# Windowed attention with an FFN behind it: global rows of two head pairs in one pass, early w_in sums column by column, loads on a second queue

## The chip, the cores and the metric

The kernel runs on one core of a Trainium2 chip. Its time is the device time of one execution in microseconds (us); lower is better. A core has a matrix engine (TensorE, PE in the profile), three engines for elementwise work (VectorE or DVE, ScalarE or ACT, GpSimd or POOL) and SyncE (SP), which here only issues DMAs. ScalarE can issue DMAs too, in its own stream of instructions; the profile calls that part of the stream ACTq. Results of TensorE land in eight PSUM banks.

## The reference

For 8 batches and 8 heads of dimension 64 there are 512 local and 32 global tokens. Scores are scaled by 1/8. A global token attends to all 544 keys, a local one to the 32 global keys and to local keys at most 32 positions away:

```python
s_g = scale * np.matmul(q_g, k_all.transpose(0, 1, 3, 2))
out_g = np.matmul(sm(s_g), v_all)
s_ll = np.where(np.abs(pos[:, None] - pos[None, :]) <= 32, s_ll, -1e9)
out_l = np.matmul(sm(np.concatenate([s_lg, s_ll], -1)), np.concatenate([v_g, v_l], 2))
...
x = attn_out.transpose(0, 2, 1, 3).reshape(B * S, H * D)     # 4352 x 512
h = x @ w_in                                                  # 512 x 2048
out = (h - np.tanh(h)) @ w_out                                # 2048 x 512
```

sm subtracts the row's maximum, exponentiates and divides by the row's sum (plus 1e-9). The weights arrive as 64-bit floats.

## The kernel before

**How the order is made.** Every piece of work is an operation of the class `Order` (L51): a function that emits instructions, the engines it may run on with a duration for each, the keys it reads and writes, the banks it takes, and a due time. `Order.run` places the operations one after another on a model of the engines and emits the instructions in the order of their planned starts. The due times come from a table of numbers (`CFG`), with a shift for single operations (`NUDGE`), a preference for one engine (`CHOICE`) and a delay (`HOLD`). The chip's own time is not known to it; on the chip each engine goes through its list in order and waits on semaphores. Where the plan has TensorE wait, before about 72 us of its own clock, it puts in filler matmuls (L1947), small and of no use for the result, which keep TensorE's clock up.

**The stages.** Batch 0's attention runs first, by pairs of heads (class `Pair`, pairs 0 to 3). For a pair, queries and keys are loaded as rows (L620), turned by TensorE (L636) and copied out of PSUM (L449): keys in windows into `first_kw`, queries into `first_q`, with the global keys put between (copies from `first_g`). Then come the scores of the 64 global rows of the pair (L669, L670), their peak on VectorE (L674, a sum with a mask and a minimum), exponentials on ScalarE (L679, L680), the inverse of the sum on VectorE (L458, L459) and the scaling on POOL. The local rows follow in windows: scores (L731), peak on VectorE (L1234), exponentials on ScalarE (L1241), scaling on POOL (L808), turning (L751), copies into `keys_first`, and the product with the values (L827), whose result is split in a high and a low part `x_hi`, `x_lo` for one column block of 128 features per pair.

From batch 1 on (class `WindowPair`, pair 4 and later) scores are made in another layout (L964, L980), with peak L1057, exponentials L1065, turning L1118. The FFN of a batch is interleaved with the attention of the next. One of its 16 steps makes 128 hidden columns: `x @ w_in` as three products of parts (hi·hi, lo·hi, hi·lo), each of four matmuls of 128x512 (L1294), then tanh on ScalarE, subtraction on VectorE, a split in parts, and four output tiles from `w_out` (L1342). After the last batch only the rest of the FFN runs.

**The weights.** They are loaded in 512 KB pieces of 64-bit floats into staging tiles (`stage`, `wpair`, `first_q`, and half pieces into `first_kw`; L521), rebuilt into 32 bits by ScalarE (L528) and VectorE (L532, L536), and split into a high part (a cast, L449) and a low part (POOL, L542). This runs beside batch 0's attention and the first steps of the FFN.

**The queues.** All loads are issued by SP, but for one half of pair 0's keys and of its queries, which ScalarE issues (L620). Each load takes the next of eight completion counters (DMAHW0 to DMAHW7 in the order's rows) and waits for the load that had that counter before.

## Time and profile before

| | us |
|---|---|
| median of 3 runs | 903.67 |
| lowest and highest | 902.84, 904.29 |
| profiled execution | 905.04 |
| its span, first to last instruction | 903.2 |

| engine | busy us | share of the span | instructions |
|---|---|---|---|
| PE (matmul) | 887.3 | 98% | 7678 |
| DVE | 648.7 | 72% | 2309 |
| ACT | 406.1 | 45% | 1186 |
| POOL | 321.0 | 36% | 511 |

The shares are means over stages that differ. TensorE's share hides what its busy time holds: fillers count as busy. The granted clock of TensorE is 0.998 over the span. The views used below are the busy time by stretches, the timelines of the engines, groups of instructions by line and shape, and the chain of waits, which goes back from the last instruction from each step to what released it.

### The profile page before, as it was taken

Reading aid. Unit: us, or ns where it says so; the run is one execution under the profiler, and the core shown is the slowest. Engines: PE = TensorE matmul, PEld = TensorE weight load, DVE = VectorE, ACT = ScalarE, POOL = GpSimd, SP = SyncE. Lnnn points to the kernel's source line nnn. Section 1 sums busy time; section 2 is a strip of 40 time slices with the busy share of each in tenths; the row PEclk is TensorE's granted clock in tenths of the full one; section 3 lists DMA queues with packets and bytes.
Section 4 is the critical chain, followed back from the end, with each engine's and each line's share of the span. In section 5 each row is a group of like instructions: output and inputs, shape, how many; then the busy total and the mean of one; then the engine's idle time right before and its main releaser. Section 6 shows DMA issues by size and latency. Waiting matters only on the chain.

```text
span 903.2 us, 21527 instructions
## 1 busy us (share of the span) xinstructions
PE 887.3 (98%) x7678; PEld 733.1 (81%) x7678; DVE 648.7 (72%) x2309; ACT 406.1 (45%) x1186; POOL 321.0 (36%) x511
## 2 busy tenths in 40 slices
PE   7899999999999999999999999999999999999998
PEld 5678878888888888888888888888888888899886
DVE  5997867776667757577775757577775758787773
ACT  6985656533334334334444334334444343443332
POOL 6677665433333413333333323333333323000000
PEclk9999999999999999999999999999999999999999
DMA  9766646533324323333333323333333210100001
GB/s 225 190 179 183 189 107 150 128 66 60 71 51 108 70 47 68 92 66 71 66 66 94 63 49 71 86 73 64 65 65 100 55 29 15 47 1 0 1 1 70
DMA packets 266058, 72.20 MB, mean 80 GB/s; under 512 B 250592, under 2 KB 259296, under 8 KB 265952
## 3 DMA queue, kind: packets, MB, share of 16 engines
q1 hardware_dynamic: 264752, 70.44, 34.2%
q8 instruction: 61, 1.00, 0.5%
q10 hardware_dynamic: 1200, 0.39, 0.2%
q14 instruction: 45, 0.37, 0.1%
HBM read 61.87 MB, written 8.91 MB: 78 GB/s over the span
## 4 chain that ended last, share of the span: by engine, by line
PE 90%; DMA 2%; DVE 2%; issue 2%; POOL 2%; ACT 1%; SPq 0%; POOLq 0%; DVEq 0%; ACTq 0%
PE bank L1342 32%; PE bank L1294 31%; PE bank L1664 7%; PE bank L1784 6%; PE bank L1151 6%; PE bank L964 3%; PE bank L980 1%; DMA wpair<-in_moe_w_out_dram 1%; PE bank L1690 1%; DMA first_q<-in_moe_w_in_dram 1%; PE bank L1947 1%; POOL w_out_lo L542 0%; DVE first_q L536 0%; POOL w_in_lo L542 0%; DMA first_raw<-in_k_l_dram 0%
## 5 line engine op out<-in xcount | busy, mean ns | idle before, releaser
L1311 POOL TENSOR_TENSOR glo<-t,ghi 128x512 fp32r<-128x512 f32 x112 | 146.4, 1307 | 285.2 <-PE bank L1342 260.7
L1096 DVE STREAM_TRANSPOSE keys_first<-prob 32x256 f32<-32x256 f32 x384 | 167.3, 436 | 8.0 <-POOL prob L1078 1.3
L1302 ACT ACTIVATE t<-bank 128x512 f32<-128x512 f32 x112 | 66.8, 596 | 164.6 <-PE bank L1294 163.3
L1305 DVE TENSOR_TENSOR t<-bank,t 128x512 f32<-128x512 f32 x112 | 76.5, 683 | 79.2 <-ACT t L1302 77.8
L449 ACT CAST ghi<-t 128x512 fp32r<-128x512 f32 (+1 forms) x122 | 74.8, 613 | 114.6 <-PE bank L1342 95.5
L1342 PE MATMUL bank<-w_out_hi,glo 128*128 128x512 f32 x448 | 124.9, 393 | 0.0
L1342 PE MATMUL bank<-w_out_lo,ghi 128*128 128x512 f32 x448 | 124.9, 393 | 0.0
L1342 PE MATMUL bank<-w_out_hi,ghi 128*128 128x512 f32 x448 | 123.5, 390 | 0.0
L1294 PE MATMUL bank<-x_hi,w_in_hi 128*128 128x512 f32 x448 | 119.9, 390 | 0.9 <-ACT w_in_hi L449 0.9
L1294 PE MATMUL bank<-x_hi,w_in_lo 128*128 128x512 f32 x448 | 120.0, 390 | 0.1
L1294 PE MATMUL bank<-x_lo,w_in_hi 128*128 128x512 f32 x448 | 120.0, 389 | 0.1
L1078 POOL TENSOR_SCALAR prob<-prob,st 128x128 f32<-128x128 f32 x224 | 81.8, 387 | 106.9 <-ACT prob L1065 90.9
L1057 DVE CUSTOM_DVE_ANT_0 prob<-bank,wraw 128x128 f32<-128x128 f32 x224 | 53.6, 286 | 89.5 <-PE bank L964 88.7
L1342 PEld LDWEIGHTS bank<-w_out_lo,ghi 128*128 128x128 f32 x448 | 83.0, 188 | 20.8 <-issue 4.3
L1342 PEld LDWEIGHTS bank<-w_out_hi,glo 128*128 128x128 f32 x448 | 83.0, 188 | 20.4 <-issue 3.7
L1294 PEld LDWEIGHTS bank<-x_hi,w_in_hi 128*128 128x128 f32 x448 | 83.7, 188 | 19.2 <-ACT w_in_hi L449 1.4
L1294 PEld LDWEIGHTS bank<-x_lo,w_in_hi 128*128 128x128 f32 x448 | 84.1, 188 | 17.9 <-DVE x_lo L838 0.5
L1342 PEld LDWEIGHTS bank<-w_out_hi,ghi 128*128 128x128 f32 x448 | 83.9, 188 | 18.0 <-issue 0.3
L1294 PEld LDWEIGHTS bank<-x_hi,w_in_lo 128*128 128x128 f32 x448 | 83.9, 188 | 18.0 <-POOL w_in_lo L542 0.6
L1065 ACT ACTIVATE prob<-prob,st 128x128 f32<-128x128 f32 x224 | 87.7, 399 | 2.6 <-DVE st L1057 1.3
L449 ACT CAST x_hi<-bank 128x256 fp32r<-128x256 f32 x59 | 19.4, 376 | 95.4 <-PE bank L980 93.6
L1151 PEld LDWEIGHTS bank<-keys_first,values 128*64 128x64 f32 x784 | 49.2, 138 | 9.9 <-DVE t L1305 7.8
(234 smaller groups left out, 1382.9 us busy)
## 6 DMA issues: line engine op xcount, KB each, us to landing
rawkq<-in_q_l_dram SPq DMA_DIRECT2D x112, 64.0 KB, 2.2
rawkq<-in_k_l_dram SPq DMA_DIRECT2D x112, 64.0 KB, 2.3
out_dram<-wpair SPq DMA_DIRECT2D x28, 256.0 KB, 2.1
values<-in_v_l_dram SPq DMA_DIRECT2D x28, 120.0 KB, 2.3
keys_first<-in_v_l_dram SPq DMA_DIRECT2D x28, 120.0 KB, 2.6
stage<-in_moe_w_out_dram SPq DMA_DIRECT2D x6, 512.0 KB, 3.9
wpair<-in_moe_w_out_dram SPq DMA_DIRECT2D x6, 512.0 KB, 4.4
first_q<-in_moe_w_in_dram SPq DMA_DIRECT2D x6, 512.0 KB, 4.9
```

Source lines behind the costliest of these rows:

```text
L449: (nc.scalar.copy if e == "A" else nc.vector.tensor_copy)(dst, src)
L1065: nc.scalar.activation(x, x, AF.Exp, bias=s[:, k:k + 1], scale=-1.0, accum_out=s[:, 8 + k:9 + k])
L1078: nc.gpsimd.tensor_scalar(x, x, s[:, k:k + 1], 1.0, op0=ALU.mult, op1=ALU.mult)
L1096: nc.vector.transpose(view(win_kf[W * k:W * k + W], [(CH, 2), (P, NT), (1, W)], 3 * G + W * i), src)
L1151: nc.tensor.matmul(dst, win_values[h][:, window(b)], src, start=n == 0, stop=n == len(parts) - 1, skip_group_check=True)
L1294: nc.tensor.matmul(self.h[s][:, j * n:(j + 1) * n], w[:, cc, f * P:(f + 1) * P], self.x()[xi][:, cc, :n], start=part == 0 and cc == 0 and ...
L1302: nc.scalar.activation(tt_[q], self.h[s], AF.Tanh)
L1305: nc.vector.tensor_sub(tt_[q], self.h.pop(s), tt_[q])
L1311: eng[e].tensor_sub(gg[q][1], tt_[q], f32(gg[q][0]))
L1342: nc.tensor.matmul(self.acc[tt], g[:, j * self.n + tt * P:j * self.n + (tt + 1) * P], low_out(f) if wi else high_out(f), start=s == 0 and ...
L1664: nc.tensor.matmul(self.hold(tt, tags), g(), low_out(f) if wi else high_out(f), start=first and k < len(tts), stop=last and k == len(mms) - 1)
L1784: nc.tensor.matmul(dst[:, at], w, m, start=fresh and n == 1, stop=n == 6, skip_group_check=True)
```

## The change

Three things change in what is computed when, and all the tables of the planner.

1. **Global rows of two pairs at once.** Pairs 0 and 1, and pairs 2 and 3, share one pass: both are turned first, their scores go to the two halves of the rows of the same two banks, and peak, exponentials, inverse and scaling are done once on 128 rows instead of twice on 64.
2. **Early sums.** For the first three steps of batch 0's FFN the twelve matmuls are not ordered by part but by column block: three matmuls for each pair, as soon as that pair's part of x is there. Two of the three take a bank of the group "acc" (4 to 7) instead of "h" (0 to 3).
3. **A second queue.** Loads of keys and queries of pairs 1 to 3, of values of batch 0 and of weights may be issued by ScalarE's queue as well; the planner chooses.

Line numbers move by up to 36: L636 becomes L648, L669 L683, L731 L749, L827 L845, L964 L982, L980 L998, L1118 L1136, L1294 L1340 for the early sums, L1947 L1983, L521 L533, L528 L540.

```diff
+    AHEAD = 3
-    CFG = dict(win=-59.4186, a_g=0.122, a_kg=0.185, a_ph=0.0132, a_qs=11.4846, a_w=0.0464, a_wn=0.0881, a_xg=7.3446, d_g=0.2172,
+    CFG = dict(win=-838.608, a_g=0.7258, a_kg=0.0055, a_ph=0.2148, a_qs=0.9626, a_w=0.056, a_wn=2.3603, a_xg=7.3446, d_g=0.7129,
...
+    def queue(e):
+        return nc.scalar if e == "A" else nc.sync
+
+    def queues(d):
+        return [("S", d), ("A", d + 0.15, CFG["a_ld"])]
...
-                nc.sync.dma_start(raw.bitcast(I32).rearrange("p (a c) k -> p a (c k)", a=a), src)
+                queue(e).dma_start(raw.bitcast(I32).rearrange("p (a c) k -> p a (c k)", a=a), src)
...
-        add(("S", 0.37), load, due, w=keys, res=spare, xfer=0.9 * N / 256)
+        add(queues(0.37), load, due, w=keys, res=spare, xfer=0.9 * N / 256)
...
-                add(("S", 0.95), load(a, (k_l, q_l)[a]), self.due(self.C["o_ld"] - 8), w=[self.key[a]], xfer=1.3)
+                add(queues(0.95) if self.j else ("S", 0.95), load(a, (k_l, q_l)[a]), self.due(self.C["o_ld"] - 8), w=[self.key[a]], xfer=1.3)
...
         def add_global_scores(self):
+            i = 2 * self.j
+            two = (self, pairs[self.j + 1])
...
+            def mm(x):
+                def fn(e, tags):
+                    if x is self:
+                        box["s0"], box["s1"] = bank([P, 256], tags[names[0]]), bank([P, 320], tags[places[0]])
+                    rows, kw = slice(64 * x.u, 64 * x.u + 64), first_kw[x.set]
+                    q = first_gq[:, x.jj].rearrange("p h g -> p (h g)")
+                    nc.tensor.matmul(box["s0"][rows], q, kw[:, :256], start=True, stop=True)
+                    nc.tensor.matmul(box["s1"][rows], q, kw[:, KG:KG + 320], start=True, stop=True)
+                return fn
...
-                for c0, c1, src, low, k in ((0, 256, box["s0"][rows], view(first_mask[rows], [(0, 256)]), 20), (256, 576, box["s1"][rows], first_mask[rows], 21)):
+                for c0, c1, src, low, k in ((0, 256, box["s0"], view(first_mask, [(0, 256)]), 20), (256, 576, box["s1"], first_mask, 21)):
...
+            early = s < AHEAD and self.name == "b0"
+
+            def column(cc):
+                def fn(e, tags):
+                    if cc == 0:
+                        self.h[s] = bank([P, 512], tags[hk])
+                    for wi, xi in ((0, 0), (0, 1), (1, 0)):
+                        nc.tensor.matmul(self.h[s], (w_in_hi, w_in_lo)[wi][:, cc, s * P:(s + 1) * P], self.x()[xi][:, cc, :n],
+                                         start=cc == 0 and wi + xi == 0, stop=cc == NCC - 1 and wi == 1)
+                return fn
+
+            for cc in range(NCC * early):
+                r = [k + (xi,) for k in self.xkeys if k[2] // 2 == cc for xi in range(2)] + [("w", "i", s, j, wi) for j in range(2) for wi in range(2)]
+                last = cc == NCC - 1
+                add(("T", 0.68), column(cc), due + 0.1 * cc - CFG["ahead"] * (not last), r=r, w=[hk],
+                    res=[tk] if last else (), alloc=[(hk, "acc" if s < 2 else "h")] if cc == 0 else ())
...
     def attention(j):
         p = pairs[j]
-        p.add_turn()
-        p.add_global_scores()
+        if j % 2 == 0:
+            p.add_turn()
+            pairs[j + 1].add_turn()
+            p.add_global_scores()
```

The order changes everywhere in the first part of the program; over the whole of it TensorE has 92 fillers before and 52 after. Three places follow. In the rows the line comes first, then the operation, out<-in and the shape of the result, in brackets the engines or completion counters waited for (Activation is ScalarE), and x4 is a row four times.

ScalarE's list from the start of the program to the first exponentials of a window (L1241), before; L528 is the rebuilding of a weight piece, L679 the exponentials of pair 0's global rows:

```order
L620 DMA first_raw<-in_k_l_dram 128x4x64
L620 DMA first_raw<-in_q_l_dram 128x4x64
L449 ACT_TABLE_LOAD
L449 COPY first_g<-bank_96 128x128 [waits PE_49]
...
L449 COPY first_kw<-bank_97 128x2x96 [waits PE_49]
L449 COPY first_kw<-first_g 128x2x2x32 [waits Activation_49]
L449 COPY first_kw<-first_g 128x2x2x32
L528 ACTIVATE stage<-stage 128x512 [waits DMAHW2_49]
L679 ACTIVATE pg<-pg,st_91 64x32 [waits DVE_49]
...
L1241 ACTIVATE t_67,st_91<-t_67,st_91 128x224 [waits DVE_49] x2
```

And after, where those are L1259:

```order
L632 DMA first_raw<-in_k_l_dram 128x4x64
...
L533 DMA wpair<-in_moe_w_out_dram 128x1024
L632 DMA first_raw<-in_k_l_dram 128x4x64
L632 DMA first_raw<-in_k_l_dram 128x4x64 [waits DMAHW0_49]
...
L455 COPY first_g<-bank_96 128x128 [waits PE_49]
...
L533 DMA first_q<-in_moe_w_in_dram 128x4x256 [waits DMAHW0_49]
L533 DMA stage<-in_moe_w_in_dram 128x4x256 [waits DMAHW3_49]
L455 COPY first_kw<-first_g 128x2x2x32 [waits Activation_49]
L1274 DMA values<-in_v_l_dram 96x3x64 [waits DMAHW5_49]
L1274 DMA values<-in_v_l_dram 96x3x64 [waits DMAHW6_49]
L1276 DMA values<-in_v_g_dram 32x6x64 [waits DMAHW7_49]
L1259 ACTIVATE t_67,st_91<-t_67,st_91 128x224 [waits DVE_49] x2
```

Five loads stand ahead of the first copy, two more ahead of the copy of pair 0's global keys (`first_kw<-first_g`), three loads of values ahead of the first exponentials; the second copy for pair 0 went to VectorE, and the exponentials of the global rows come later.

TensorE's list at the start, from the last turn of pair 0 (the queries) on, before; L669 and L670 are pair 0's global scores, L636 turns pair 1's keys, L731 makes window scores:

```order
L636 MATMUL bank_98<-idr,first_raw 128x128 [waits DMAHW5_49,DMAHW2_49]
...
L669 MATMUL bank_99<-first_kw,first_m 64x256 [waits DVE_49,Activation_49]
L670 MATMUL bank_100<-first_kw,first_m 64x320
L636 MATMUL bank_101<-idr,first_raw 128x128 [waits DMAHW1_49,DMAHW0_49]
...
L731 MATMUL bank_102<-first_kw,first_q 128x224 [waits DVE_49]
...
```

And after, the same work at L648, L683, L684 and L749:

```order
L648 MATMUL bank_98<-idr,first_raw 128x128 [waits DMAHW7_49,DMAHW2_49]
...
L683 MATMUL bank_99<-first_kw,first_m 64x256 [waits DVE_49,Activation_49]
L684 MATMUL bank_100<-first_kw,first_m 64x320
L749 MATMUL bank_101<-first_kw,first_q 128x224 [waits DVE_49]
...
L648 MATMUL bank_97<-idr,first_raw 128x128 [waits DMAHW6_49,DMAHW0_49]
...
L648 MATMUL bank_98<-idr,first_raw 128x128 [waits DMAHW2_49,DMAHW1_49]
...
L683 MATMUL bank_99<-first_kw,first_m 64x256 [waits DVE_49]
L684 MATMUL bank_100<-first_kw,first_m 64x320
...
```

The window scores of pair 0 now come ahead of pair 1's turns, and pair 1's global scores directly behind these, in the same two banks as pair 0's.

TensorE's list from pair 4's last global scores (L980) to the turn of its probabilities (L1118), before; L827 is the last product of batch 0, L1294 the sums of the FFN's first steps:

```order
L980 MATMUL bank_98<-first_m,win_gq 32x192
L827 MATMUL bank_102<-keys_first,values 64x160 [waits DMAHW2_49,DMAHW0_49]
...
L1947 MATMUL bank_97<-mask_88 128x224
L1294 MATMUL bank_97<-x_hi_85,w_in_hi 128x512 x3
L1294 MATMUL bank_97<-x_hi_85,w_in_hi 128x512 [waits Activation_49]
L1294 MATMUL bank_96<-x_hi_85,w_in_hi 128x512 [waits DVE_49]
L1294 MATMUL bank_96<-x_hi_85,w_in_hi 128x512 x3
...
L1294 MATMUL bank_97<-x_hi_85,w_in_lo 128x512 x4
L1294 MATMUL bank_96<-x_lo_86,w_in_hi 128x512 x4
L1118 MATMUL bank_98<-idr,prob 128x64 [waits Pool_49]
```

And after, with L998, L845, L1340 and L1136 for them; the second product of the two stands among the sums:

```order
L998 MATMUL bank_98<-first_m,win_gq 32x192
L1340 MATMUL bank_103<-x_hi_85,w_in_hi 128x512
L1340 MATMUL bank_103<-x_lo_86,w_in_hi 128x512 [waits DVE_49]
...
L1340 MATMUL bank_98<-x_hi_85,w_in_hi 128x512 [waits DVE_49,Activation_49]
...
L1340 MATMUL bank_98<-x_hi_85,w_in_lo 128x512 [waits Pool_49]
L845 MATMUL bank_100<-keys_first,values 64x160 [waits DMAHW5_49,DMAHW3_49]
...
L1340 MATMUL bank_98<-x_hi_85,w_in_hi 128x512
L1340 MATMUL bank_98<-x_lo_86,w_in_hi 128x512
...
L1340 MATMUL bank_98<-x_hi_85,w_in_hi 128x512
...
L1340 MATMUL bank_103<-x_hi_85,w_in_lo 128x512
L1983 MATMUL bank_97<-mask_88 128x224
L1136 MATMUL bank_97<-idr,prob 128x64 [waits Pool_49]
```

Before has twenty matmuls of the FFN between these two places and none earlier; after has nine, three and nine, and twelve more, not shown, ahead of pair 4's window scores (L982).

## Rows read from the trace of the kernel before

**Rows 1.** Stretches: length, busy us of PE, PEld, DVE, ACT, POOL; PEclk, DMA share, GB/s.

```profile
5.00:12.00 7.00, 6.55 (x28) 4.46 (x30) 2.20 (x11) 4.16 (x12) 4.58 (x19) 1.00 1.21 287
12.00:22.00 10.00, 8.86 (x77) 6.14 (x75) 9.33 (x37) 8.57 (x31) 5.17 (x10) 1.00 1.03 231
42.00:55.00 13.00, 11.76 (x155) 8.94 (x162) 12.53 (x45) 10.78 (x35) 10.69 (x16) 0.87 0.72 182
72.00:120.00 48.00, 46.92 (x339) 37.72 (x337) 36.37 (x94) 30.22 (x69) 32.65 (x34) 1.00 0.65 174
203.00:303.00 100.00, 100.00 (x936) 82.11 (x936) 71.40 (x275) 40.05 (x128) 35.53 (x59) 1.00 0.34 71
```

**Rows 2.** The chain of waits, one long run (start, us, what).

```profile
313.36 5.44 PE bank L1294 x24
```

**Rows 3.** Line L1947, the fillers, in the first 62 us.

```profile
0.00:62.00 62.00, 11.77 (x92) 8.91 (x92) 0.97 0.84 203
```

**Rows 4.** TensorE's timeline (start, us, engine, line, operation, count, idle before).

```profile
7.39 1.11 PE L669 MATMUL bank<-first_kw,first_m 128*64 128x256 f32 x2
54.71 1.16 PE L964 MATMUL bank<-first_m,hi 64*32 64x128 f32 x64
65.20 0.71 PE L1118 MATMUL bank<-idr,prob 64*128 64x64 f32 x16
114.55 1.20 PE L1294 MATMUL bank<-x_hi,w_in_hi 128*128 128x512 f32 x4 [0.94 <-ACT w_in_hi L449]
```

**Rows 5.** VectorE, groups by line and shape to 57 us (busy, mean ns | idle).

```profile
L674 DVE CUSTOM_DVE_ANT_0 pg<-bank,first_mask 64x256 f32<-64x256 f32 x4 | 1.7, 422 | 0.7 <-PE bank L669 0.6
L674 DVE CUSTOM_DVE_ANT_0 pg<-bank,first_mask,st 64x320 f32<-64x320 f32 x4 | 2.2, 550 | 1.1 <-PE bank L670 0.6
L459 DVE RECIPROCAL st<-st 64x1 f32<-64x1 f32 x4 | 0.6, 158 | 0.1
L458 DVE TENSOR_REDUCE st<-st 64x1 f32<-64x2 f32 x4 | 0.6, 146 | 0.3 <-ACT pg L680 0.3
L449 DVE COPY keys_first<-bank 128x512 f32<-128x512 f32 x5 | 3.4, 673 | 0.4 <-PE bank L751 0.4
L449 DVE COPY first_kw<-bank 128x384 f32<-128x384 f32 x2 | 1.1, 540 | 0.0
L532 DVE TENSOR_SCALAR stage<-stage 128x512 int32<-128x512 int32 x5 | 2.7, 542 | 0.0
L536 DVE SCALAR_TENSOR_TENSOR stage<-stage 128x512 int32<-128x512 int32 x5 | 3.7, 745 | 0.0
```

**Rows 6.** ScalarE, groups by line and shape to 57 us.

```profile
L680 ACT ACTIVATE pg<-pg,st 64x576 f32<-64x576 f32 x4 | 3.1, 773 | 0.2
L679 ACT ACTIVATE pg<-pg,st 64x32 f32<-64x32 f32 x4 | 1.3, 319 | 0.3
L528 ACT ACTIVATE stage<-stage 128x512 f32<-128x512 f32 x5 | 3.5, 692 | 1.9 <-DMA stage<-in_moe_w_out_dram 1.9
```

**Rows 7.** VectorE's timeline, first window peak.

```profile
11.99 0.39 DVE L1234 CUSTOM_DVE_ANT_0 t<-bank,mask 128x224 f32<-128x224 f32 x1 [1.10 <-PE bank L731]
```

**Rows 8.** ScalarE's timeline (ACTq: its queue of DMA issues).

```profile
1.25 0.52 ACTq L620 DMA_DIRECT2D first_raw<-in_q_l_dram  x1
7.03 0.51 ACT L449 COPY first_kw<-first_g 128x128 f32<-128x128 f32 x2
9.41 0.68 ACT L528 ACTIVATE stage<-stage 128x512 f32<-128x512 f32 x1 [1.88 <-DMA stage<-in_moe_w_out_dram]
```

**Rows 9.** SP's timeline of DMA issues.

```profile
4.90 0.50 SPq L521 DMA_DIRECT2D stage<-in_moe_w_out_dram  x1
106.57 0.55 SPq L521 DMA_DIRECT2D first_q<-in_moe_w_in_dram  x1
```

**Rows 10.** The tile stage in the first 20 us.

```profile
DMA to landing us min/median/max: 4.5/5.1/5.7
```

**Rows 11.** The chain of waits, pair 1's first turn.

```profile
9.57 1.05 PE bank L636 x4
```

More of the change, by code (lines that the diff above doesn't have):

```diff
@@ L619, in fn @@
                     for h in range(2):
-                        (nc.scalar if h and self.j == 0 else nc.sync).dma_start(first_raw[self.set][:, a, :, h],
+                        (nc.scalar if h and self.j == 0 else queue(e)).dma_start(first_raw[self.set][:, a, :, h],
                                                                              src[self.b, 2 * self.jj + h].rearrange("(t p) d -> p t d", p=P))
@@ L1255, in load @@
                 for a in range(2):
[L1256 removed]
+                    queue(e).dma_start(raw[:96, 3 * a:3 * a + 3], bass.AP(src.tensor, src.offset + 224 * D * a, [[D, 96], [96 * D, 3], [1, D]]))
                 g = v_g[self.b, self.h]
[L1258 to L1260 removed]
+                queue(e).dma_start(raw[96:], bass.AP(g.tensor, g.offset, [[D, G], [0, 6], [1, D]]))
+            add(queues(1.45), load, self.pair.due(self.C["o_vl"] + self.C["o_tw"] * self.two), w=[f"vh{self.two}"], xfer=0.95)
     step_no = [0]
@@ L1314, in add_hidden @@
             fs = range(s * self.per, (s + 1) * self.per)
-            for part in range(3):
+            early = s < AHEAD and self.name == "b0"
[12 more added lines that the diff above has]
+                    res=[tk] if last else (), alloc=[(hk, "acc" if s < 2 else "h")] if cc == 0 else ())
+            for part in range(3 * (not early)):
                 wi, xi = ((0, 0), (0, 1), (1, 0))[part]
```

72 lines of the change are left out of this document (33 added, 39 removed), and 142 rows, old and new, of tables (CHOICE, HOLD, NUDGE).

## The prediction

> **What bounds the kernel now.** I read the busy time by stretches first [rows 1]. From 203 to 303 us TensorE is busy for all of its 100 us: nothing can be gained there except by removing matmuls, and none of use is removed. One long run of the chain of waits gives their price: 24 matmuls of 128x512 take 5.44 us, 0.227 us each [rows 2]. What TensorE does not use lies at the front: of its busy time before 62 us 11.77 us are the 92 fillers of L1947, which compute nothing and take 0.128 us each [rows 3]. They stand where the planner saw TensorE wait, and those it waits for are VectorE and ScalarE: from 12 to 22 us they are busy 9.33 and 8.57 of ten, from 42 to 55 us 12.53 and 10.78 of 13 [rows 1]. So two numbers decide: when the dense stretch of these two begins and how much work it holds, and how many useful matmuls TensorE has done when pair 4's window chain lets it go on. TensorE's timeline [rows 4] fixes the places in before: global scores of pair 0 at 7.39, window scores of pair 4 (L964) at 54.71, and pair 4's probabilities turned (L1118) at 65.20 without a wait. After that the timeline has one loss of note, 0.94 us at 114.55, on a high part of w_in [rows 4]; all that is idle from 72 to 120 us is 1.08 us [rows 1].
>
> **1. The early sums: −2.95 us.** The three first w_in sums, column by column, have the same 36 matmuls as before. What counts is how many come before the turn of pair 4, from which on the stream is dense. Counted in the order, before has 20 between L964 and L1118, and none earlier. After has 12 ahead of pair 4's window scores, and 9 + 3 + 9 between these and the turn: 33. The 13 more fill time in which TensorE waited or ran fillers: 13 x 0.227 = 2.95 us [rows 2]. If pair 4's chain (54.71 to 65.20) stays as long as it was, this is gained whole. The cover is that chain: were it gone, the early matmuls would be worth nothing, since the same work would only stand earlier. The plan itself still has fillers ahead of the turn, so there is time there.
>
> **2. Global rows of two pairs in one pass, and copies between engines.** In before a pair's peak on VectorE takes 0.422 + 0.550 us, its inverse 0.158 + 0.146 [rows 5]; its exponentials on ScalarE 0.773 + 0.319 [rows 6]. A pass over 128 rows has as many columns, and I take it as equally long: a peak of 128x224 takes 0.39 us [rows 7], 1.7 ns a column, as do the 256 columns of 64 rows in 0.422. Pair 0's peak and exponentials lay ahead of the dense stretch; in it before has three of each, after two. By the order, between the first window peak and that of pair 4, VectorE loses a peak (−0.97), two inverses (−0.61), a 512-column copy (−0.67) and of the weights' rebuilding a piece (−0.54 − 0.75) and one first step (−0.54), against half a piece more (+0.64); it gains a K-window copy (0.54, and 0.3 for its smaller part, worked out from that) and a copy of global keys (+0.26, half of ScalarE's 0.51 for two [rows 8]). Sum −2.3 us [rows 5]. ScalarE loses one set of exponentials (−1.09), the K-window copy (−0.84, at VectorE's price) and the global copy (−0.26), and gains the 512-column copy (+0.67, at VectorE's price), one and a half pieces' rebuilding (1.5 x 0.69 = +1.04) less half a cast (−0.34, at the same price), and one DMA issue (+0.5): −0.3 us [rows 6, 8].
>
> **3. ScalarE's queue: the stretch begins later, +2.3 us.** In before ScalarE issues two small loads, the second at 1.25, and has made its share of pair 0's global keys by 7.54 [rows 8]. In after it issues five loads, one of 512 KB, then copies the first globals, and then two more 512 KB loads stand ahead of its copy for pair 0, both with a wait: loads use eight completion counters in turn, and a load waits for the one that had its counter before. The second of the two waits for the w_out piece that SP loads into the stage buffer. In before that piece was issued at 4.90 [rows 9], and its rebuilding, which waited for it, began at 9.41 [rows 8]; loads into this buffer took 4.5 to 5.7 us [rows 10], so 9.4 to 10.6. Then come an issue of 0.5 us and the copy of 0.3 [rows 8]: pair 0's global scores start at 10.3 to 11.6, I take 10.7, against 7.39, +3.3. Pair 1's first turn, 1.05 us at its pace [rows 11], now stands behind pair 0's window scores and not ahead of them. So the first window peak, 11.99 before [rows 7], comes at 14.25: +2.3 (bounds +1.9 and +3.2).
>
> The DMA share is 1.21 from 5 to 12 us and 1.03 from 12 to 22 [rows 1], with nearly everything issued by SP, so I count nothing gained by a second issuer. The Trainium skill, "DMA: Bandwidth & Descriptors", section "Issuing engines are not separate DMA queues", speaks against this part of the change too: DMAs of several issuers end on the same 16 engines and interleave, and only the sequencer's time to issue is saved. The trace agrees as far as it shows the full share.
>
> **4. From the stretch's begin to pair 4: +1.0 us.** If VectorE sets the pace all through, pair 4's window scores slip by 2.3 − 2.3 = 0; if ScalarE does, by 2.3 − 0.3 = +2.0. In the stretches of [rows 1] each is near full, VectorE the more by up to 1.8 us in 13, but ScalarE's exponentials stand between VectorE's peaks and inverses; I take the middle.
>
> **5. Weights later: −0.6 us.** In before SP issues a long block of pair 5's values ahead of the w_in load at 106.57 [rows 9], and the 0.94 us at 114.55 is the wait for that piece. In after these values stand earlier, and TensorE needs the piece later relative to pair 4's turn. It can't be better than −1.1, all that is idle there [rows 1], and a new order of loads can make a wait of half the old one, +0.5. TensorE's order in the tail is unchanged.
>
> **The sum:** −2.95 + 1.0 − 0.6 = −2.55. The profiled execution took 905.04 us (span 903.2), so 902.5 for one like it; the median of the runs is 1.37 lower, 903.67, so **901.1 us**. The terms' ends give −2.95 + 0 − 1.1 = −4.05 and −2.95 + 2.0 + 0.5 = −0.45, or 899.6 to 903.2. A cross-check: the order has 52 fillers in place of 92, 40 x 0.128 = −5.1 [rows 3], against which stand 3.3 of bare wait at the start; with the −0.6 that is −2.4.
>
> **Rivals.**
> - *A, ScalarE does not stall at its loads.* Pair 0's global keys come on time and term 3 is zero: −2.95 − 1.3 (the middle of −2.3 and −0.3) − 0.6 = −4.85, 898.8. For it: the loads that ScalarE issues in before's start [rows 8] wait for nothing, so no row shows such a stall. Against it: the order writes the waits out, and ScalarE's instructions run one behind the other.
> - *B, the weights set the pace.* The 512 KB pieces are rebuilt by VectorE, ScalarE and POOL beside the first FFN steps; TensorE, ahead by 13 matmuls, reaches a piece sooner, and the lead of 2.0 to 2.5 us comes back as waits from 66 to 115 us. The 0.94 of before shows how little slack there is; that after's order needs the pieces later speaks against it. About 0: 903.7.
> - *C, slower.* Place: ScalarE from 5 to 30 us. The first peak comes at the upper bound, +3.2; ScalarE sets the pace, −0.3; and its later loads stop it while exponentials queue behind: three loads of values, each with a wait, stand directly ahead of the first exponentials, and a load of w_in waits among them. I price these by the one wait for a load that ScalarE's rows show, 1.88 us [rows 8]. 3.2 − 0.3 + 1.88 − 2.95 = +1.83: 905.5. It decides once pair 4's window scores slip by more than 2.95 us.
>
> **How the numbers follow.** About 0.2% (1.8 us) is what a measurement of this kernel can tell from no change. Chances: forecast 0.45, A 0.12, B 0.23, C 0.20. Of the forecast's own range 0.33 lies beyond −1.8 and 0.12 within; A is faster; B gives 0.03 faster, 0.17 same, 0.03 slower; C 0.16 slower, 0.04 same. Faster 0.48, same 0.33, slower 0.19. The range 898.7 to 905.0 takes in A, B and C's lower part.
>
> **What would show it.** Right: TensorE's global scores near 10.7 us, after a wait for ScalarE; the first window peak near 14; window scores of pair 4 between 54.7 and 56.7; 33 sums of the FFN done at the turn, itself at 65 to 67 us; no wait near 1 us after that. Wrong: scores at 7 to 8 us (A); waits on parts of w_in or w_out of over 1.5 us in all from 66 to 115 us (B); window scores of pair 4 after 57.7 (C); or a chain from these to the turn longer than 10.5 us, by which the lead is lost where I count it as gained.

## The result, and the profile after

The changed kernel takes 913.61 us (median of 4 runs, 912.77 to 914.12) against 903.46 of the kernel before beside it: a ratio of 1.0104, 95% interval 1.0089 to 1.0119. It is 1% slower, where 0.3% faster was forecast. The profiled execution has a span of 912.1 us; before had 903.2. (The medians differ by 10.2 us and the spans by 8.9, since before's profiled execution was 1.6 us above this median of its runs and the changed kernel's 0.3 above its own.)

TensorE's timeline answers to [rows 4] (columns as there):

```profile
8.91 1.97 PE L648 MATMUL bank<-idr,first_raw 128*128 128x128 f32 x8 [4.03 <-DMA first_raw<-in_k_l_dram]
13.93 1.11 PE L683 MATMUL bank<-first_kw,first_m 128*64 128x256 f32 x2 [3.05 <-ACT first_kw L455]
...
60.02 1.16 PE L982 MATMUL bank<-first_m,hi 64*32 64x128 f32 x64
...
68.67 0.47 PE L1340 MATMUL bank<-x_hi,w_in_hi 128*128 128x512 f32 x1 [1.04 <-ACT w_out_hi L455]
...
71.57 1.26 PE L1136 MATMUL bank<-idr,prob 64*128 64x64 f32 x16
...
93.26 0.40 PE L982 MATMUL bank<-first_m,hi 64*32 64x128 f32 x2 [0.40 <-DVE t L1323]
93.86 1.03 PE L982 MATMUL bank<-first_m,hi 64*32 64x128 f32 x55 [0.20 <-DVE t L1323]
...
101.10 1.45 PE L1312 MATMUL bank<-x_hi,w_in_hi 128*128 128x512 f32 x4 [1.93 <-DVE xg L1206]
```

Pair 0's first turn, its global scores, pair 4's window scores and their turn stand at 8.91, 13.93, 60.02 and 71.57; before they stood at 5.32, 7.39, 54.71 and 65.20. Behind the turn, up to 120 us, there are three waits for VectorE, of 0.40, 0.20 and 1.93 us, where before had one of 0.94 at 114.55. By stretches, as in [rows 1]:

```profile
5.00:12.00 7.00, 1.97 (x8) 1.43 (x8) 1.83 (x6) 0.87 (x4) 4.54 (x20) 1.00 1.11 267
12.00:22.00 10.00, 7.03 (x30) 4.60 (x31) 4.06 (x26) 3.79 (x16) 0.00 (x0) 1.00 0.74 184
72.00:120.00 48.00, 45.35 (x330) 36.15 (x327) 35.41 (x100) 29.45 (x65) 34.88 (x34) 0.96 0.70 180
102.00:104.00 2.00, 2.00 (x6) 1.57 (x5) 1.99 (x5) 1.81 (x8) 0.11 (x1) 0.50 0.57 130
```

From 5 to 22 us VectorE is busy for 1.83 and 4.06 us (2.20 and 9.33 before), ScalarE for 0.87 and 3.79: the dense stretch begins late. The last row shows TensorE at the lower of its clock levels, 1.2 GHz: behind the 1.93 us of waiting the granted clock was 0.5 for 3.4 us (101.8 to 105.2). ScalarE's timeline, against [rows 8], shows why the begin is late:

```profile
1.79 0.53 ACTq L533 DMA_DIRECT2D wpair<-in_moe_w_out_dram  x1
...
11.15 0.37 ACTq L533 DMA_DIRECT2D first_q<-in_moe_w_in_dram  x1
13.16 0.37 ACTq L533 DMA_DIRECT2D stage<-in_moe_w_in_dram  x1
13.58 0.30 ACT L455 COPY first_kw<-first_g 128x128 f32<-128x128 f32 x1 [7.69 <-DMA stage<-in_moe_w_out_dram]
```

The 512 KB piece into `wpair` goes out at 1.79, with pair 0's own keys and queries; the loads at 11.15 and 13.16 waited, and the copy behind them (7.69 us of idle time, put down to a load into `stage`) is the one that the global scores at 13.93 needed. The landings of the first 20 us (KB each, median us to landing):

```profile
stage<-in_moe_w_out_dram SPq DMA_DIRECT2D x1, 512.0 KB, 7.5
...
first_raw<-in_k_l_dram ACTq DMA_DIRECT2D x3, 128.0 KB, 7.0
```

The load into `stage` went out at 5.62 and took 7.5 us, which lies outside the 4.5 to 5.7 of [rows 10]; it landed at 13.1, and the load that ScalarE had to wait with went out at 13.16. VectorE's first window peak, against [rows 7]:

```profile
18.07 0.39 DVE L1252 CUSTOM_DVE_ANT_0 t<-bank,mask 128x224 f32<-128x224 f32 x1 [5.59 <-PE bank L749]
```

And the fillers, against [rows 3] (to 80 us here), of which 52 are left, as the order had it:

```profile
0.00:80.00 80.00, 6.03 (x52) 4.52 (x52) 0.96 0.74 177
```

For the experiments one number is worked out from each trace: the useful matmuls begun up to a time, each weighed with its pace in a dense stretch (0.227 us for 128x512). The lag says how much later than in the kernel before the same work is reached; the times are those of before.

| lag, us, at | 20 | 65 | 75 | 85 | 98 | 120 | 850 |
|---|---|---|---|---|---|---|---|
| changed kernel | 6.7 | 0.7 | 4.0 | 4.0 | 8.4 | 7.2 | 8.9 |
| every load on SP | 0.0 | −4.9 | −1.4 | −1.4 | 3.2 | 1.9 | 3.6 |
| sums at the last pair | 6.0 | 8.5 | 9.8 | 9.8 | 9.5 | 8.8 | 10.5 |
| every load on SP, sums at the last pair | 0.3 | 4.2 | 5.5 | 5.5 | 5.0 | 3.8 | 6.7 |
| every load on SP, half transfers | 0.0 | −5.6 | −2.4 | −2.4 | −2.8 | −4.0 | −1.1 |

(One trace each. Executions of one of these kernels differ by 1.3 to 5.8 us; before's own profiled execution was 1.4 us above the median of its first three, and that of the fourth row 2.6 above its median. The entries at 65 hang on the weights of the small matmuls by up to 1.0 us, the others by 0.2. Steps within a row say more than its end.)

So the changed kernel is late by 6.7 us at 20 us, has made nearly all of it good at 65 by the early sums, stands at 4.0 behind the turn, loses 4.4 more between 85 and 98, gets 1.2 back where before had its own wait, and loses the rest later.

### The profile page after: what moved, and what is told of

Same layout as the page of the kernel before. It is cut to its first block, busy times and chain, and to the rows that moved or that the text cites. A ratio compares the mean times of both kernels' runs of the same rounds, so it can differ in the third digit from the quotient of the medians.

```text
span 912.1 us, 21398 instructions
## 1 busy us (share of the span) xinstructions
PE 887.5 (97%) x7638; PEld 731.5 (80%) x7638; DVE 652.5 (72%) x2314; ACT 401.7 (44%) x1166; POOL 319.2 (35%) x506
## 3 DMA queue, kind: packets, MB, share of 16 engines
HBM read 61.87 MB, written 8.91 MB: 78 GB/s over the span
## 4 chain that ended last, share of the span: by engine, by line
PE 88%; DMA 4%; DVE 4%; ACT 1%; issue 1%; POOL 1%; SPq 1%; ACTq 0%; DVEq 0%; POOLq 0%
PE bank L1376 33%; PE bank L1312 32%; PE bank L1700 7%; PE bank L1820 6%; PE bank L1169 6%; PE bank L982 3%; DMA stage<-in_moe_w_out_dram 1%; PE bank L998 1%; PE bank L1726 1%; DMA first_kw<-in_moe_w_in_dram 1%; DMA wpair<-in_moe_w_out_dram 1%; DMA first_q<-in_moe_w_in_dram 1%; DVE stage L548 1%; DMA values<-in_v_l_dram 0%; DMA first_raw<-in_q_l_dram 0%
## 5 line engine op out<-in xcount | busy, mean ns | idle before, releaser
L455 ACT CAST ghi<-t 128x512 fp32r<-128x512 f32 (+1 forms) x112 | 68.8, 614 | 125.0 <-DVE t L1323 106.7
L1312 PE MATMUL bank<-x_hi,w_in_hi 128*128 128x512 f32 x436 | 117.2, 391 | 1.9 <-DVE xg L1206 1.9
L1312 PE MATMUL bank<-x_lo,w_in_hi 128*128 128x512 f32 x436 | 117.4, 391 | 0.0
L1312 PE MATMUL bank<-x_hi,w_in_lo 128*128 128x512 f32 x436 | 117.1, 390 | 0.0
L1312 PEld LDWEIGHTS bank<-x_hi,w_in_hi 128*128 128x128 f32 x436 | 81.7, 188 | 19.8 <-ACT wpair L540 2.3
L1169 PE MATMUL bank<-keys_first 128*64 128x32 f32 (+2 forms) x784 | 54.6, 228 | 0.0
```

What stands on the lines that cost most here:

```text
L455: (nc.scalar.copy if e == "A" else nc.vector.tensor_copy)(dst, src)
L1169: nc.tensor.matmul(dst, win_values[h][:, window(b)], src, start=n == 0, stop=n == len(parts) - 1, skip_group_check=True)
L1312: nc.tensor.matmul(self.h[s][:, j * n:(j + 1) * n], w[:, cc, f * P:(f + 1) * P], self.x()[xi][:, cc, :n], start=part == 0 and cc == 0 and ...
```

## The experiments

Times are medians; ratios are to the kernel before on the same chip, with the 95% interval. Two theories stood against each other: **Q**, that the loads on ScalarE's queue cost the start, and **W**, that the weight pieces set the pace from 65 us on.

### The second queue

Every load by SP, in the planned order:

```diff
 def queue(e):
-    return nc.scalar if e == "A" else nc.sync
+    return nc.sync
```

> The changed kernel with every load issued by SP, in the planned order; nothing else differs. Theory Q (the loads on ScalarE's queue cost the start: a 512 KB piece issued at 1.79 us takes transfer time from pair 0's keys and queries, and ScalarE stops at loads that wait): TensorE's first turn of pair 0 at 5.3 us instead of 8.9, first window peak before 13 instead of 18.07, pair 4's window scores near 55 instead of 60.02, and 905 to 908 us. Theory W (the weight pieces set the pace from 65 us on; there the work done lags before by only 0.7 us): the start comes early just the same, but TensorE waits that much longer at the weights between 66 and 105 us, and the time stays at 911 or more.

Measured: 907.97 us, ratio 1.0042 (1.0027 to 1.0056), 5.6 less than the changed kernel. TensorE's timeline:

```profile
5.62 1.94 PE L648 MATMUL bank<-idr,first_raw 128*128 128x128 f32 x8 [0.53 <-DMA first_raw<-in_k_l_dram]
...
53.65 1.16 PE L982 MATMUL bank<-first_m,hi 64*32 64x128 f32 x64
...
65.77 1.27 PE L1136 MATMUL bank<-idr,prob 64*128 64x64 f32 x16
...
88.04 0.40 PE L982 MATMUL bank<-first_m,hi 64*32 64x128 f32 x2 [0.57 <-DVE t L1323]
...
95.85 1.51 PE L1312 MATMUL bank<-x_hi,w_in_hi 128*128 128x512 f32 x4 [1.90 <-DVE xg L1206]
```

The first turn is back at 5.62, pair 4's window scores come earlier than in the kernel before (54.71), and at the turn more work is done, as Q says. But the waits for VectorE stay (0.57, 0.20, 1.90), which leaves W open, with its place at 88 to 96 us.

Only the first piece moved from ScalarE to SP, behind pair 1's queries (the operation with number 84):

```diff
-        for _, _, fn, e, args in out:
-            fn(e, args)
+        for _, i, fn, e, args in out:
+            fn("S" if i in (84,) else e, args)
```

> The changed kernel with one load moved: the first 512 KB piece of w_out (into wpair) is issued by SP behind pair 1's queries instead of by ScalarE at 1.79 us. If that piece is what delays pair 0's loads (theory Q, first half): first turn of pair 0 at 5.3 us, global scores near 10.7, some 3 us earlier than 13.93, and 910 to 911 us. If pair 0's loads are late for another reason (many loads at once on two queues): first turn still after 8 us and 913 to 914. Theory W: 912 to 914 whatever the start does.

Measured: 908.88 us, ratio 1.0058 (1.0041 to 1.0076). TensorE's timeline of this kernel:

```profile
6.09 2.29 PE L648 MATMUL bank<-idr,first_raw 128*128 128x128 f32 x8 [1.29 <-DMA first_raw<-in_k_l_dram]
9.34 1.12 PE L683 MATMUL bank<-first_kw,first_m 128*64 128x256 f32 x2 [0.96 <-ACT first_kw L455]
```

One load moved gives 4.7 us back. The first turn stands at 6.09 and the global scores at 9.34, with 0.96 us of wait for ScalarE left of 3.05. So most of ScalarE's stop goes with the piece: it lasts as long as the transfers that it waits for.

Only the two waiting pieces and the three loads of values that stood ahead of ScalarE's copy and first exponentials moved to SP (numbers 66, 78 and 34 in the same line):

> The changed kernel with the five loads that stand ahead of ScalarE's copy and of its first exponentials (two 512 KB pieces of w_in, three loads of values) issued by SP, and the first piece of w_out still by ScalarE at 1.79 us. If ScalarE's stop at them costs by itself (theory Q, second half): first turn of pair 0 still near 8.9 us, but its global scores near 10.8 instead of 13.93, first window peak near 15, and 910 to 911 us. If the stop lies wholly beside the late loads of pair 0: global scores after 13 and 913 to 914. Theory W: 912 to 914.

Measured: 909.91 us, ratio 1.0073 (1.0058 to 1.0088). TensorE's first turn in it:

```profile
8.56 2.20 PE L648 MATMUL bank<-idr,first_raw 128*128 128x128 f32 x8 [3.65 <-DMA first_raw<-in_k_l_dram]
```

The first turn is nearly as late as in the changed kernel, but the global scores follow at 10.69 without a wait (13.93 there), and 3.7 us are gained: the stop costs by itself. The two gains (4.7 and 3.7) overlap, since the run with every load on SP, which takes in both, gives 5.6.

The piece alone, in the kernel before: the second piece of w_out issued by ScalarE behind its first two loads.

```diff
-        for _, _, fn, e, args in out:
-            fn(e, args)
+        for _, i, fn, e, args in out:            # 78 is planned at 2.2 for this
+            fn("A" if i == 78 else e, args)
```

> The kernel before with one load moved: the 512 KB piece of w_out into wpair, which SP issues at 5.45 us, is issued by ScalarE behind its two first loads, near 1.8 us. Theory Q, first half (the piece takes transfer time from pair 0's keys and queries): first turn of pair 0 near 8 us instead of 5.32, window scores of pair 4 later than 54.71 by 2 us or more, 905.5 to 907 us. If SP's own loads are not held up by a piece on the other queue: first turn before 6 us and 903 to 904.

Measured: 906.54 us, ratio 1.0036 (1.0023 to 1.0050). TensorE's first turn, pair 4's window scores and their turn:

```profile
8.17 1.94 PE L637 MATMUL bank<-idr,first_raw 128*128 128x128 f32 x8 [3.36 <-DMA first_raw<-in_k_l_dram]
...
56.75 1.16 PE L965 MATMUL bank<-first_m,hi 64*32 64x128 f32 x64
...
67.25 0.71 PE L1119 MATMUL bank<-idr,prob 64*128 64x64 f32 x16
```

A load on a second queue, which takes no issue time on SP's, delays the small loads issued beside it: the half of pair 0's keys that SP issues at 1.66 lands 6.4 us after its issue, where it took 3.5 before, and the first turn comes 2.85 us later (5.32 before). Pair 4's window scores and their turn are 2.0 us later (54.71 and 65.20 before). In this trace most of that is made good by 118 us, where the wait of 0.94 in [rows 4] is gone: 0.4 us of lag are left. The medians differ by 2.8 all the same (906.54 against 903.78); the profiled execution (905.71) is the fastest of the six, and where the others lose more is not known.

### The early sums

The twelve matmuls of each early sum emitted at the last column block, in the changed kernel:

```diff
+                    if cc < NCC - 1:
+                        return
+                    for part, (wi, xi) in enumerate(((0, 0), (0, 1), (1, 0))):
+                        for c in range(NCC):
```

> The changed kernel with the twelve matmuls of each of the three early w_in sums emitted together where the last pair's part stood, so that none comes ahead of pair 4's window scores. If term 1 is right (2.95 us for 13 matmuls at 0.227): 916 to 917 us. If TensorE has free time ahead of the turn of pair 4 that these matmuls would fill as well (2.4 us of waiting and fillers there in the changed kernel): 914 to 915. If the early sums hold back pair 4's chain: 912 or less.

Measured: 915.45 us, ratio 1.0140 (1.0119 to 1.0162): 1.85 more than with early sums by the medians, 3.3 by the ratios. The early sums are worth something, but these runs can't tell 1.85 from the forecast 2.95. TensorE's timeline, with the turn in the second row:

```profile
67.05 0.77 PE L1343 MATMUL bank<-x_hi,w_in_hi 128*128 128x512 f32 x1 [2.94 <-ACT w_out_hi L455]
...
75.96 0.71 PE L1136 MATMUL bank<-idr,prob 64*128 64x64 f32 x16
```

TensorE now waits 2.94 us in one piece at 67.05. The row puts it down to a cast of w_out, which this matmul does not read; what it does read is pair 3's part of `x_hi`, and VectorE's cast of that ended 0.15 us before it (66.90). The lag at 75 us is 5.8 larger than in the changed kernel (9.8 against 4.0), and at 98 us 1.1 (9.5 against 8.4). Pair 5's window scores at 98.63 follow without a wait. So in these traces most of what the early sums gave by 75 us they had lost again by 98.

The same with every load on SP:

> As the run with every load on SP (907.97 us), with the twelve matmuls of each early w_in sum emitted together where the last pair's part stood. With two queues this made the time 1.85 us longer, and in the trace TensorE then lagged by 5.8 us more at 70 us and gave 4.4 of that back by 98 us, where it found the weights ready. If the weights set a floor near 98 us: again a large lag at 70 us (3 us or more behind the run with every load on SP), no wait for VectorE near 96, and 908 to 909.5 us. If the early sums count whole: 910.9 or more (2.95 us for 13 matmuls).

Measured: 909.13 us, ratio 1.0063 (1.0046 to 1.0081), 1.2 more than with early sums by the medians, 1.9 by the ratios, with intervals that overlap. The same places in TensorE's timeline:

```profile
63.92 0.76 PE L1343 MATMUL bank<-x_hi,w_in_hi 128*128 128x512 f32 x1 [4.35 <-ACT w_out_hi L455]
...
71.57 0.71 PE L1136 MATMUL bank<-idr,prob 64*128 64x64 f32 x16
...
94.26 1.16 PE L982 MATMUL bank<-first_m,hi 64*32 64x128 f32 x64
```

Again a lag of 6.9 more at 75 us (5.5 against −1.4), of 1.8 at 98, and no wait at 94.26. Something near 98 us takes the lead away, wherever it was won; it is called the floor from here on. (At 850 us the two rows are 3.1 apart again, so what the early sums are worth at the end stays open.) The wait of 4.35 is the same one as above, for pair 3's part of `x_hi`, as VectorE's timeline of this kernel shows:

```profile
63.35 0.41 DVE L455 CAST x_hi<-bank 128x256 fp32r<-128x256 f32 x1
```

### What the floor is

Values for pair 4 moved behind four weight pieces in SP's list (emission only; the base of this and of the next ones is the kernel with every load on SP, 907.97):

```diff
+        out = [({353: 79.6}.get(v[1], v[0]),) + v[1:] for v in out]
         out.sort(key=lambda v: (v[0], v[1]))
```

> As the run with every load on SP (907.97 us), and the block of 16 loads of values for pair 4 moved in SP's list from ahead of four weight pieces to behind them; nothing else. There the pieces were issued at 75.64 to 80.92 us, behind the block (64.90 to 75.5), and VectorE, busy rebuilding them, held TensorE for 1.90 us at 95.85, after which the granted clock fell to half for 3.4 us in that profile. If the block holds the weights up: pieces issued from 66 on, the wait at 96 below 0.5 us, no half clock there, 904 to 906 us. If their buffers hold them up (the loads also wait for POOL): issued after 75 all the same, and 907 to 909. If the values now come too late: a new wait of 1 us or more at pair 4's product near 85 us, and 908 to 910.

Measured: 911.71 us, ratio 1.0092 (1.0077 to 1.0107). Two issues in SP's timeline of this kernel:

```profile
63.63 0.45 SPq L534 DMA_DIRECT2D stage<-in_moe_w_out_dram  x1
...
75.39 0.35 SPq L534 DMA_DIRECT2D wpair<-in_moe_w_out_dram  x1
```

and of TensorE:

```profile
87.55 0.35 PE L1170 MATMUL bank<-keys_first 128*64 128x96 f32 x2 [2.46 <-DMA keys_first<-in_v_g_dram]
```

The third answer: the values come too late, TensorE waits 5.35 us in four pieces for them. On the way it shows what holds the pieces. The first of the four, whose buffer was free, went 12.0 us earlier (63.63 against 75.64). The other three went only 2.8 to 3.8 us earlier, although SP was free from 66 us on: the one into `wpair` was issued at 75.39, when POOL was done with the buffer (78.84 with the values ahead of it).

Two steps of VectorE's rebuilding moved behind the low parts of pair 4's output:

```diff
+        out = [({287: 91.2, 380: 93.46}.get(v[1], v[0]),) + v[1:] for v in out]
```

> As the run with every load on SP (907.97 us), and in VectorE's list two first steps of rebuilding a weight piece (L544) moved behind the low parts of pair 4's output (L1202, L1206) that they stood ahead of; nothing else. In that run the step on the stage tile took 1.32 us at 93.94, and TensorE waited 1.90 us, to 95.85, for what came behind it. If VectorE's order at this place makes the wait: wait below 0.8 us, and with it no half clock behind it: 905 to 906.7 us. If the weights themselves set the pace there (late loads, whatever the order of VectorE): TensorE waits as long in all between 88 and 106 us, on a part of w_in or w_out in place of xg, and 907.5 to 908.5.

Measured: 906.74 us, ratio 1.0039 (1.0026 to 1.0053); the interval overlaps that of its base. TensorE's timeline, at the place of the 1.90:

```profile
93.03 1.17 PE L1313 MATMUL bank<-x_hi,w_in_hi 128*128 128x512 f32 x4 [0.67 <-DVE xg L1207]
```

The wait falls from 1.90 to 0.67 as expected and those at 88 us are gone, but the time falls by 1.2 at most: a new wait comes at 105 us (0.80 for probabilities), and at 157 us there are 1.39 where the base had 1.13 at 160.

The same two steps moved, and only the early loads (to 25 us) taken from ScalarE's queue:

```diff
+            fn("S" if i in (84, 13, 66, 78, 34, 409) else e, args)
```

> The changed kernel with the loads that ScalarE issues in the first 25 us (pair 1's keys, four weight pieces, three loads of values) issued by SP, the four later weight pieces still by ScalarE, and the two steps of VectorE behind pair 4's low parts as in the run before (906.74 us). With every load on SP TensorE had a new wait of 1.13 us near 160 us (1.39 in the run with the two steps moved), which the changed kernel did not have. If only the early loads hurt on ScalarE's queue: no such wait near 160, and 904.5 to 906 us, still behind the kernel before or level with it. If the later loads on ScalarE cost as much as they save: 906.5 to 908.

Measured: 907.53 us, ratio 1.0048 (1.0030 to 1.0066). The number is the one of the second answer, the place is that of neither, as TensorE's timeline shows:

```profile
108.35 1.35 PE L1313 MATMUL bank<-x_hi,w_in_hi 128*128 128x512 f32 x4 [1.90 <-ACT w_in_hi L456]
```

The wait near 160 is gone, 0.64 are left at 92.95, and one of 1.90 us on a part of w_in stands at 108.35.

The second rebuilding step left out for six pieces (their weights are then not rebuilt):

```diff
+            if i not in (231, 300, 225, 237, 288, 381):
+                fn(e, args)
```

> As the run with every load on SP (907.97 us), and for the six weight pieces that VectorE rebuilds between 77 and 100 us the second step (L548, 0.7 us each) left out, so that these pieces of the weights are not rebuilt; the loads, ScalarE's step, the casts and POOL's part stay. It takes 4 us of work from VectorE there. If VectorE's share of the rebuilding sets the floor on which the lead is lost: the waits of 0.77 and 1.90 us at 88 and 96 us fall below 1 us together, no half clock follows, and 904 to 905.5 us. If the pieces' transfers and buffers set it: TensorE waits for a cast of a piece in the same place, and 907 to 908.5.

Measured: 908.21 us, ratio 1.0054 (1.0042 to 1.0066), no better than its base. TensorE's timeline:

```profile
106.16 1.20 PE L1313 MATMUL bank<-x_hi,w_in_hi 128*128 128x512 f32 x4 [1.09 <-ACT w_in_hi L456]
```

Some 4 us less work for VectorE, and the waits shrink and move: 0.69 for VectorE at 92, 1.09 for a cast of w_in at 106. The chain of waits that ends at 106.16 still runs through three loads (into `first_q` at 77.60, `wpair` at 86.94 and `stage` at 99.26, 5.2 to 5.6 us each), with ScalarE and POOL between them. So VectorE's share alone does not set the floor. It is not free of it either: in this trace, the fastest of the six executions, only about 1 us is lost from 85 to 98, against 4.6 in its base's, though the median shows no gain.

Transfers halved: pieces planned from 44 to 100 us loaded for 64 of 128 partitions (the other half keeps old values).

```diff
+                rows = P // 2 if HALF[0] else P
-                queue(e).dma_start(raw...rearrange("p (a c) k -> p a (c k)", a=a), src)
+                queue(e).dma_start(raw...rearrange("p (a c) k -> p a (c k)", a=a)[:rows], src[:rows])
```

> As the run with every load on SP (907.97 us), with the weight pieces whose load is planned from 44 to 100 us loaded for 64 of the 128 partitions only, so that half of each such piece keeps old values; everything else stays, the rebuilding too. If transfers and buffers set the floor on which the lead is lost: loads land in some 3 us instead of 5, the waits of 0.77 and 1.90 us at 88 and 96 us fall below 1 us together without a half clock behind them, and 903 to 905.5 us. If they don't (the order in which the engines work sets it): the waits stay, 907 to 908.5.

Measured: 904.34 us, ratio 0.9992 (0.9981 to 1.0004): level with the kernel before, 0.5% below its base by the ratios. The turn of pair 4 and the next window scores in TensorE's timeline:

```profile
65.14 1.27 PE L1141 MATMUL bank<-idr,prob 64*128 64x64 f32 x16
...
86.36 1.16 PE L987 MATMUL bank<-first_m,hi 64*32 64x128 f32 x64
```

and the landing of loads issued from 60 to 110 us (KB each, median us), first with every load on SP and whole pieces, then here:

```profile
stage<-in_moe_w_out_dram SPq DMA_DIRECT2D x3, 512.0 KB, 5.1
...
first_q<-in_moe_w_in_dram SPq DMA_DIRECT2D x2, 512.0 KB, 4.7
```

```profile
stage<-in_moe_w_out_dram SPq DMA_DIRECT2D x3, 256.0 KB, 3.7
...
first_q<-in_moe_w_in_dram SPq DMA_DIRECT2D x2, 256.0 KB, 4.5
```

With half the bytes the landing is sooner by 0.2 us into `first_q`, by 1.4 into `stage` and by 1.5 into `wpair` (5.0 to 3.5). Over the chain this adds up: two pieces that are issued at 88.17 and 100.06 in the base are issued at 83.38 and 96.09 here. The waits at 88 to 96 us are gone, and with them the stretch at half the clock: the mean granted clock over the span of the profiled execution is 1.000. The control, the kernel before with the same halved loads:

> The kernel before with the same pieces (load planned from 44 to 100 us) loaded for half of the partitions only. It has one wait on a weight piece there, 0.94 us at 114.55. Theory of the floor: before does not stand on it, so the gain is at most that wait, 902.5 to 904 us against 903.6. If halved transfers help any kernel at the front by relieving the other loads: 902 or less, and then the same gain in the changed order would show nothing.

Measured: 903.34 us, ratio 0.9994 (0.9983 to 1.0005): no gain clear of noise, where the changed order gained 0.5%. So the transfers of the weights are part of the floor, and the kernel before stands on it with no more than its 0.94.

How they act is seen in the chain of waits, taken from 60 to 125 us. In the changed kernel it goes back from the matmul behind the wait of 1.93 to VectorE, and from there through three loads of weights (start, us, what):

```profile
64.51 5.58 DMA wpair<-in_moe_w_out_dram
...
76.06 4.15 DMA stage<-in_moe_w_out_dram
...
85.50 5.24 DMA first_q<-in_moe_w_in_dram
...
100.83 0.13 DVE xg L1206
...
101.10 7.29 PE bank L1312 x24
```

Between the loads stand the rebuilding on ScalarE and VectorE and, before the third, SP's own list of loads (80.23 to 85.50). With every load on SP the chain is of the same kind: a load into `wpair` at 58.88, rebuilding, POOL's low parts up to 79.2, by which buffers come free, a load into `first_q` at 80.44, VectorE, and the matmul at 95.85. With half transfers (55 to 110 us) it is TensorE alone behind this row:

```profile
66.14 0.27 PE bank L1141 x2
```

So W holds from 70 us on. The floor is the cycle of loading a piece, rebuilding it and freeing its buffer, with SP's list as a part of it; how much each part has is not shown. Up to 90 us 22 weight loads have landed in the kernel before, 18 in the changed kernel, 20 with every load on SP and 22 with half transfers (24, 20, 22 and 22 are issued). At 70 us the kernel before, the changed kernel and the one with every load on SP had all issued 16, so the shortfall comes from 70 to 90 us.

### Two more

The joint global rows done in halves, peak, exponentials, inverse and scaling twice on 64 rows:

```diff
+            halves = [slice(0, 64), slice(64, 128)]
+                for r in halves:
```

> As the run with every load on SP (907.97 us), with peak, exponentials, inverse and scaling of the joint global rows done twice on 64 rows instead of once on 128, in the same places. By the prediction's durations that adds 2 x (0.97 + 0.30 and two readings of 0.08) = 2.9 us to VectorE and 2 x 1.09 = 2.2 and two readings to ScalarE ahead of pair 4. If these engines pace the front: pair 4's window scores near 56 instead of 53.65, and 910 to 911 us. If the passes lie in idle time: below 54.2 and 907.5 to 908.5.

Measured: 907.51 us, ratio 1.0049 (1.0032 to 1.0067), the same as its base. TensorE's timeline at pair 4's window scores:

```profile
54.99 1.16 PE L988 MATMUL bank<-first_m,hi 64*32 64x128 f32 x64
```

Pair 4's window scores come 1.3 us later than in its base (53.65), so the passes do lie in a busy stretch, but nothing of it reaches the end. That the floor takes it is a reading: its trace still has 1.93 us of wait for VectorE, at 95.03.

The planner offered SP alone:

```diff
-        return [("S", d), ("A", d + 0.15, CFG["a_ld"])]
+        return ("S", d)
```

> The changed kernel with its three kinds of load offered to SP alone, so that the planner makes its whole order anew under that rule, with the same tables. In its order TensorE has 92 fillers again. If the tables' order is good once the second queue is gone: 901 to 905 us, below the 907.97 of the changed order with all loads moved to SP. If the numbers were fitted to the order with two queues and fit no other: 908 or more, with waits of its own before 65 us.

Measured: 924.39 us, ratio 1.0235 (1.0205 to 1.0264). The tables do not fit this order, and nothing follows for the queue. No version tried beats the kernel before clear of noise.

## Why the prediction was wrong

**Part 3 was mis-sized, and a mechanism was left out of it.** The first window peak came 6.1 us later (11.99 to 18.07), not 2.3. The step that failed is the price of the wait: it took from the kernel before that pair 0's own loads come on time, that the piece into `stage` goes out at 4.90 and that it takes 4.5 to 5.7 us. I took the full share of the DMA engines only as a reason against a gain. But a 512 KB piece issued at 1.79 takes time from whatever is loaded beside it: pair 0's first turn moved by 3.6 us, a term that the sum did not have, and the piece into `stage` went out at 5.62 and took 7.5. The Trainium skill ("DMA: Bandwidth & Descriptors", section "Issuing engines are not separate DMA queues") says that DMAs of several issuers run on the same engines and interleave. The run of the kernel before with that one load moved (first turn 2.85 us later) agrees. ScalarE's stop was foreseen, with its place and its load. (The bounds 10.3 and 11.6 are 0.1 and 0.2 above the terms they are added up from, which changes nothing.) Rival A was excluded by the 7.69 us of idle time.

**Parts 2 and 4 came near, in part by luck.** From the first window peak to pair 4's window scores the time shrank from 42.72 to 41.95 us, by 0.8, where 2.3 − 1.0 = 1.3 was forecast. In this stretch VectorE's busy time fell by 2.4 us (40.94 to 38.55), as forecast, but ScalarE's by 2.2 (38.49 to 36.25), where 0.3 was; and VectorE was idle for 3.4 us of it, against 1.8. So with less work on both engines the stretch shrank by less than either: the middle that I took was near for another reason than the one given. A pass over 128 rows is as long as one over 64, as assumed; VectorE's peak, against [rows 5, 6]:

```profile
L689 DVE CUSTOM_DVE_ANT_0 pg<-bank,first_mask 128x256 f32<-128x256 f32 x2 | 0.8, 412 | 0.0
L689 DVE CUSTOM_DVE_ANT_0 pg<-bank,first_mask,st 128x320 f32<-128x320 f32 x2 | 1.1, 550 | 0.3 <-DVE st L689 0.2
```

and of ScalarE:

```profile
L695 ACT ACTIVATE pg<-pg,st 128x576 f32<-128x576 f32 x2 | 1.6, 776 | 0.1
```

**Part 1 was right in its count; its worth stays open.** 33 matmuls came ahead of the turn. The chain to it grew from 10.5 to 11.55 us, with 1.04 us of wait among the early sums themselves. The row puts this down to a cast of w_out, but the matmul reads pair 3's part of `x_hi`, whose cast on VectorE ended 0.14 us before it (68.53): the last column block has to wait for the last pair, and the cover was not whole. Leaving the early sums out raised the lag at 75 us by 5.8 and 6.9 us, of which 1.1 and 1.8 were left at 98. In the time it cost 1.85 and 1.2 us by the medians, 3.3 and 1.9 by the ratios, which does not exclude 2.95.

**Part 5 had the wrong sign.** The wait that it counted on losing was lost: 1.2 us of lag went where before had its 0.94. But 4.4 us were lost from 85 to 98 us (in before's time): 0.40 + 0.20 + 1.93 us of waits, and about 1.7, an estimate, for 3.4 us at half the clock. The failed step is the upper end of +0.5, "a new order of loads can make a wait of half the old one", with "TensorE needs the piece later relative to pair 4's turn" behind it: I compared when one piece is needed, and did not count how many have come by then (18 landed against 22 by 90 us). This is rival B in its mechanism, with a price above its 2.0 to 2.5, since a slower clock came with the wait. Its sign did not show as written, though: TensorE waited not on parts of w_in or w_out but on VectorE, which was late itself by the chain of loads. Rivals B and C were given as either one or the other; both came at once, C's late begin (pair 4's window scores slipped by 5.3 us, past its 2.95) and B's floor.

**The sum, with what was measured:** −2.95 (sums, as counted) + 6.1 (begin) − 0.8 (stretch) + 1.05 (chain) + 4.4 (floor) − 1.2 (before's own wait, gone) + 1.7 (later pieces, the lag from 120 to 850 us) = 8.3, against 8.9 of the span; 0.6 at the turn is not accounted for. Of the later 1.7 no single cause was looked for.

## What to carry to other kernels

Before loads go onto a second queue, look at what is in flight beside them: a queue of its own is not paced by the first. In the kernel before with one load moved, the 512 KB piece issued at 1.80 landed at 7.77, ahead of the 128 KB load that SP had issued at 1.66 (8.04). An engine that also computes should issue only loads that wait for nothing by the time it gets there: here that was worth 3.7 us. And a lead of the bounding engine is worth what the next shared supply leaves of it: count the pieces landed by that time, in both orders, before counting the lead.

## What was not expected of the hardware

A wait of 2 us in a dense stretch can cost nearly twice its length: behind 1.93 us the granted clock was 0.5 for 3.4 us. It does not follow every time. Of six kernels with one wait of 1.90 to 1.99 us between 95 and 109 us, the clock fell to 0.5 behind it in three (the changed kernel, the one with every load on SP, the one with only the early loads on SP) and stayed at 1.0 in three (the head piece on SP, the waiting loads on SP, the rows in halves); what tells them apart is not known. And halving the bytes of 512 KB loads shortened their landing by only 0.2 to 1.5 us (`first_q` 4.7 to 4.5, `wpair` 5.0 to 3.5), yet that was enough, over a chain of such loads, to take a wait of 1.9 us away.
